# Narrowing the weights four slices ahead instead of two in a recurrence and feed-forward kernel, with a new order for its first third

## The chip, the cores and the metric

The kernel runs on one core of one Trainium2 chip. The metric is device time in microseconds (us) of one execution; a time for the kernel is the median of several runs. A second kind of number comes from the profile of one single execution, whose own time is given beside its span (the stretch that the profiler's records cover).

## What is computed

A recurrence over 768 steps for 4 x 8 heads of width 40 (RWKV-7), whose output becomes the 3072 x 320 input of an RMS norm and a SwiGLU feed-forward with 1536 inner columns:

```python
batch, n_heads, seq, head_dim = (4, 8, 768, 40)
for t in range(S):
    kt, vt, rt = (k[:, :, t], v[:, :, t], r[:, :, t])
    wt, at, bt = (w[:, :, t], a[:, :, t], b[:, :, t])
    y[:, :, t] = np.einsum('bhd,bhde->bhe', rt, state)
    Sa = np.einsum('bhde,bhe->bhd', state, at)
    state_decay = state * wt[:, :, None, :] - np.einsum('bhd,bhe->bhde', Sa, bt)
    state = state_decay + np.einsum('bhd,bhe->bhde', vt, kt)
...
x = np.ascontiguousarray(attn_out.transpose(0, 2, 1, 3)).reshape(B * S, H * D)
rms = np.sqrt(np.mean(x * x, axis=-1, keepdims=True) + 1e-06)
xn = x / rms * rms_g
g = xn @ w_gate
silu = g * (1.0 / (1.0 + np.exp(-g)))
val = xn @ w_val
return (silu * val @ w_out).astype(np.float32)
```

The weights w_gate, w_val and w_out arrive as 64-bit numbers.

## The kernel before

**Tiling.** The 768 steps are cut into 24 chunks of 32. Each chunk passes three stages. `front(c)` (L652) loads w, a, k, b and v of the chunk, turns them on TensorE and builds, level by level (pieces of kind `gramk`), the triangular matrix `LT` and the scaled keys `KN` and decays. `inverse(c)` (L760), or `early_inverse(c)` (L778) for the first four chunks, inverts the triangular matrix on VectorE by a chain of small multiply and subtract pairs; the matrix goes through DRAM to change its layout, out by `sB<-LT` and in by `M<-sB` before the chain, and out by `sY<-M` (or `sY<-Yi`) and back after it. In the early form two TensorE pieces of kind `inv` follow, which need the four loads `M<-sY`. `main(c)` (L810) takes the state from chunk to chunk (kinds `state`, `lower`, `update`), forms the outputs (`score`, `level`, `y0`), and normalises them into `xg`; with `main` of an even chunk go the `rn` loads of r for two chunks.

After each second chunk `feed(g)` (L939), g = 0 to 11, applies the feed-forward to the 256 tokens of two chunks. It goes over the 12 slices f of 128 inner columns in six pairs; a pair loads two slices of weights (`wf<-sW`, 480 KB each; "load f" below), then runs the TensorE pieces `h64`, `h` and `out` with ScalarE's silu and VectorE's product in between.

**The narrowing.** The 64-bit weights become 32-bit on chip, once, while the first chunks run. `narrow_slice(f)` (L995) does slice f in two halves, stages "narrow 2f" and "narrow 2f + 1", so there are 24 halves, 0 to 23 ("half 11" is the second half of slice 5). `narrow` (L973) loads raw weights into a wide buffer by two or four DMAs, makes three ScalarE instructions and three VectorE instructions of it, and stores the result to the DRAM scratch `sW[f]`, from which all twelve groups load.

**Wide buffers.** There are WB = 5 of them, named `wf`. A turn counter gives them out in rotation, in the order in which the Python code asks: for the raw halves and for the feed loads alike. So a request waits for whatever read the buffer five requests before. In `feed(0)` the requests interleave:

```python
for f in range(LEAD if g == 0 else 0):
    narrow_slice(f)
for f in range(0, FT, 2):
    for e in range(2):
        if g == 0 and f + LEAD + e < FT:
            narrow_slice(f + LEAD + e)
```

and then the pair's two loads are asked for. With LEAD = 2 halves 0 to 7 come first, then loads 0 and 1, halves 8 to 11, loads 2 and 3, and so on; loads 8 to 11 come last.

**What sets the order.** Nothing is issued while the Python code of the stages runs. The helpers (`dve` and its kin at L442 to L489) only record a piece: its engine, its kind and what it must wait for. `Plan.issue` then issues the 6028 pieces in the order that the string ORDER (L33) spells out: each number is a piece's distance from the first one not yet issued, and "-" is a warm-up matmul (L1015), 151 in all, which keeps TensorE busy and whose result is not used. Each engine, and each of the DMA queues of SyncE (SP) and GpSimd (POOL), does its own pieces in this order and waits at each for what that piece needs. The places given below count the pieces of one engine, from 0. PAIRS (L228) says for each of 499 rooms (a use of PSUM by one result) which of three pairs of PSUM banks, `ps0` to `ps2`, it lives in; the feed-forward's output sums in `po`.

All helpers record from one line each, so most VectorE work stands under L444 in the profile, ScalarE copies under L467, scalings under L470, other ScalarE work under L464, DMAs under L483 and matmuls under L486 and L489; what tells them apart is the tile.

Of the kernel before, what the change touches and what calls it, by code (L numbers as in the profile page):

```python
# [22 lines left out]
LEAD = 2  # L23
# [10 lines left out]
85 83 84 76 58 78 86 74 73 59 60 75 5 89 61 88 77 4 43 6 201 7 87 334 90 44 8 214 213 53 62 9 - - - - - - - - 93 18 10  # L34
567 335 557 11 12 13 79 14 15 94 566 80 210 16 95 558 108 17 200 - - - 97 96 19 20 100 21 2 22 101 23 98 25 568 202 24
26 107 112 57 - - - - - 102 106 111 124 27 209 122 392 103 109 52 119 113 104 54 578 569 577 155 199 125 110 105 204
120 - - - - - - 114 203 118 117 121 559 211 598 589 562 46 131 129 132 45 560 212 597 563 588 561 123 115 136 586 384
133 134 - - - - - 126 130 116 47 564 3 145 216 394 383 135 336 128 137 48 144 143 141 91 587 219 142 51 570 127 1005
565 146 138 337 55 573 579 281 393 220 582 608 571 390 234 239 607 572 583 580 380 574 251 222 38 221 609 575 581 42 -
- - - - - - - 223 82 226 339 64 379 227 338 39 81 139 224 263 149 576 238 153 56 249 247 590 206 584 228 382 237 591  # L40
593 272 40 233 232 381 154 0 593 32 139 390 204 228 591 388 234 249 247 - - 324 235 35 31 27 244 229 146 147 259 281
245 258 149 34 325 594 36 33 270 155 243 62 605 584 598 230 - 239 40 214 599 601 242 628 64 49 91 627 602 30 626 1135
600 28 48 257 603 29 241 68 150 255 65 0 1347 194 0 194 84 173 0 - - - 182 540 200 0 184 1 186 542 540 0 506 0 457 469
849 199 455 242 111 97 110 112 96 51 61 439 460 458 122 50 243 0 0 255 242 0 709 104 470 242 120 246 259 708 57 247
458 456 0 257 718 256 470 242 0 716 265 487 486 0 268 0 0 265 101 473 0 262 277 0 273 0 236 0 260 0 269 0 242 461 - -
- - - - - 237 0 240 0 278 242 252 0 242 252 0 90 0 0 98 99 246 0 0 230 440 0 230 94 93 457 440 231 - - - - - - - - -
240 441 244 0 44 0 468 440 255 0 450 468 269 469 0 257 214 439 238 213 203 0 257 203 93 449 92 0 0 234 - - - - - - - -
245 437 0 250 262 0 464 246 247 436 260 245 446 258 259 469 244 - - 255 471 465 468 470 466 0 269 215 255 478 466 93
94 264 95 96 266 97 0 97 470 1 2 98 99 0 0 96 467 97 469 98 468 251 265 99 470 100 471 101 441 102 103 258 104 105 260
106 - - - - - - - - - - - 0 106 107 471 108 0 108 502 503 472 0 108 109 110 111 0 0 0 0 0 - - 13 0 16 562 572 146 571  # L50
561 147 14 142 143 374 15 13 355 - - - 25 386 358 0 358 386 388 16 25 387 389 390 70 79 17 391 28 191 147 355 356 80
148 149 359 0 68 28 2 29 149 0 149 34 150 29 151 187 24 25 31 152 33 153 188 391 393 32 154 35 390 392 358 0 0 152 40
187 153 27 154 155 156 33 157 158 159 160 161 34 162 36 163 164 37 165 41 391 38 42 392 39 394 561 166 395 393 552 0
42 559 549 548 395 209 0 549 560 42 165 210 43 44 211 427 428 395 - - - 565 166 45 167 557 168 0 565 566 168 739 0 522
693 534 526 124 - - 0 526 124 139 0 535 681 682 579 0 535 545 547 140 536 138 141 0 547 545 555 543 578 0 558 520 567
- - - - - - 518 378 0 696 378 380 381 695 518 120 685 526 - - - - - - 522 686 379 527 382 136 530 383 554 529 121 - -
141 540 523 565 539 537 142 538 524 - - - - 145 525 148 534 149 152 154 551 535 147 555 - - 157 146 550 536 150 155
# [3 lines left out]
478 595 568 - - 35 830 594 567 820 38 36 - 476 37 571 366 570 0 605 356 433 434 435 436 120 437 0 317 318 319 320 441  # L61
321 322 323 355 456 324 458 459 442 4 357 325 457 326 327 443 328 0 443 328 329 330 331 357 0 35 0 330 2 37 450 359 3
36 358 331 332 357 333 356 0 462 330 461 464 448 331 332 468 364 447 463 31 467 476 458 333 365 334 335 0 425 439 441
302 426 436 0 6 439 2 0 435 332 2 436 443 444 0 448 332 442 334 443 333 340 449 0 32 297 329 342 330 - 3 338 33 341
334 0 332 331 0 332 293 441 0 438 0 436 293 333 336 295 337 309 438 338 1 375 342 310 365 374 515 27 292 0 362 26 28
44 339 29 34 292 27 32 338 0 646 29 34 336 32 0 439 64 315 647 646 339 440 441 63 340 0 287 413 312 313 623 12 414 314
415 315 416 608 624 32 417 480 418 625 419 420 421 316 626 638 33 0 312 417 625 418 - - - - 476 313 601 602 600 610
812 419 420 421 822 258 422 423 0 313 810 423 625 637 2 0 819 2 0 254 473 420 421 645 310 422 0 - - - - - 310 422 3
313 33 0 28 626 307 419 639 627 420 637 308 0 637 20 635 420 647 21 421 23 422 613 648 819 38 22 809 423 39 659 24 611
3 612 36 818 424 651 808 621 425 25 660 426 - 616 249 427 0 427 3 25 58 57 428 28 47 0 428 429 28 430 3 431 0 26 25  # L70
614 484 31 27 617 627 0 458 216 400 590 600 401 0 12 582 32 401 583 25 0 397 579 21 - - - - - - - - - 588 29 28 30 591
22 453 428 398 605 23 0 591 23 429 602 24 609 0 24 397 588 602 1 604 398 429 430 2 399 427 0 584 - - - - - - - - - - -
- - - 4 397 0 25 397 4 0 393 394 21 23 27 28 395 598 24 424 607 0 21 38 35 395 37 396 24 2 424 47 397 398 399 400 25
# [4 lines left out]
663 729 634 977 562 563 717 713 986 978 665 564 565 566 975 567 568 714 569 985 570 571 967 722 572 723 - 0 400 403  # L78
726 402 572 401 573 0 726 738 736 573 739 574 664 575 737 576 577 3 723 578 751 579 760 580 747 581 582 633 583 584 0
584 585 3 634 586 636 587 635 734 588 633 0 746 588 - - - - - 403 757 589 722 590 3 404 591 592 593 594 595 596 408  # L80
# [288 lines left out]
def kernel(  # L369
# [569 lines left out]
    def feed(g):  # L939

        x = xg.pop(g)
        po = po_
# [6 lines that stand above are left out]
            plan.stage = "feed", g  # L949
# [98 lines left out]
```

## Time and profile before

| | us |
|---|---|
| three runs | 1069.33, 1063.34, 1067.66 |
| median | 1067.66 |
| the profiled execution, own time | 1062.36 |
| its span | 1060.6 |
| mean granted TensorE clock in it | 0.979 of full |
| PE busy | 1009.5 (95%) |
| PE weight load busy | 829.3 (78%) |
| DVE busy | 842.3 (79%) |
| ACT busy | 468.1 (44%) |
| POOL busy | 309.5 (29%) |

PE is TensorE, DVE is VectorE, ACT is ScalarE, POOL is GpSimd and SP is SyncE, which here does nothing but start DMAs. The profile gives for each instruction its start, its duration, the tile that it writes and reads, and what ended the idle time before it. A view by windows cuts the span and gives each engine's busy time in each piece, and the clock that TensorE was granted (1.00 is full).

The six largest groups after the matmuls are these; those with `ex`, `wf` and `sW` belong to the narrowing and the feed loads.

| group | count | busy us or median |
|---|---|---|
| PE ps<-xg,wf, the feed-forward's first product | 1728 | 353.5 us |
| PE po<-wf,hT, its second | 576 | 183.1 us |
| DVE tmp<-Yi,M and Yi<-Yi,tmp, the inverse's chain | 1240 | 260.4 us |
| DVE K<-K,T | 192 | 93.4 us |
| ACT K<-K | 168 | 71.7 us |
| DMA wf<-sW | 144 | 3.9 us from issue to landing |

### The profile page before, as it was taken

How to read it: one execution, taken by the hardware profiler on the slowest of the kernel's cores; microseconds unless marked ns; L12 is line 12 of the kernel's file. 1: busy time of each engine (PE TensorE's matmuls, PEld its weight loads, DVE VectorE, ACT ScalarE, POOL GpSimd, SP SyncE). 2: the span in 40 equal slices, each digit the busy share in tenths (PEclk: the TensorE clock that was granted, in tenths of full speed). 3: DMA queues.
4: the chain of work that ended last, by engine and by line, in shares of the span. 5: the costliest groups of instructions: out<-in, count | busy, mean ns of one | idle time of the engine just before them, and what ended most of it. 6: DMA issues, size and time to landing. Idle time of an engine off the chain costs nothing.

```text
span 1060.6 us, 53494 instructions
## 1 busy us (share of the span) xinstructions
PE 1009.5 (95%) x23406; PEld 829.3 (78%) x23406; DVE 842.3 (79%) x2861; ACT 468.1 (44%) x1043; POOL 309.5 (29%) x554
## 2 busy tenths in 40 slices
PE   7868999999999999999999999999999999999997
PEld 6767777777888778787778778787777888787875
DVE  8978878776868988898898798989889899787411
ACT  6856666643543534434443444434344443431211
POOL 8824413120532241241233241340331331110000
PEclk9777998999999999999999999999999999999999
DMA  9965458766565483655565555574555555443252
GB/s 168 216 155 133 77 127 207 211 123 178 127 140 126 106 173 96 150 134 125 123 155 129 135 132 114 122 160 119 137 126 126 138 137 138 100 132 102 80 162 68
DMA packets 172457, 143.35 MB, mean 135 GB/s; under 512 B 125504, under 2 KB 143872, under 8 KB 172224
## 3 DMA queue, kind: packets, MB, share of 16 engines
q1 hardware_dynamic: 153856, 116.96, 42.9%
q0 software_dynamic: 16192, 22.64, 12.1%
q8 instruction: 184, 3.01, 1.2%
q10 hardware_dynamic: 2176, 0.33, 0.3%
q14 instruction: 49, 0.40, 0.1%
HBM read 123.86 MB, written 15.99 MB: 132 GB/s over the span
## 4 chain that ended last, share of the span: by engine, by line
PE 72%; DVE 8%; DMA 4%; ACT 3%; issue 3%; POOL 2%; SPq 1%; DVEq 0%; ACTq 0%; POOLq 0%
PE ps L486 50%; PE po L486 13%; PE ps L489 8%; DMA wf<-sW 2%; DVE LT L444 1%; DVE y L444 1%; DVE tmp L444 1%; POOL kbn L483 1%; DVE Yi L444 1%; DVE K L444 1%; SPq L483 1%; DMA sY<-Yi 1%; ACT VU L467 1%; PE po L1015 0%; DVE Ab L444 0%
## 5 line engine op out<-in xcount | busy, mean ns | idle before, releaser
L486 PE MATMUL ps<-xg,wf 128*128 128x256 f32 (+1 forms) x1728 | 353.5, 390 | 4.0 <-DVE xg L444 2.0
L486 PEld LDWEIGHTS ps<-xg,wf 128*128 128x128 f32 (+1 forms) x1728 | 261.4, 188 | 57.2 <-issue 15.0
L486 PE MATMUL po<-wf,hT 128*128 128x320 f32 x576 | 183.1, 449 | 0.1
L464 ACT ACTIVATE sg<-ps 128x256 f32<-128x256 f32 x144 | 53.6, 382 | 228.2 <-PE ps L486 224.9
L444 DVE TENSOR_TENSOR tmp<-Yi,M 128x60 f32<-128x60 f32 (+24 forms) x620 | 130.7, 211 | 19.1 <-DMA M<-sB 5.9
L444 DVE TENSOR_TENSOR Yi<-Yi,tmp 128x60 f32<-128x60 f32 (+24 forms) x620 | 129.7, 209 | 12.7
L483 POOL DMA_DIRECT2D VU<-in_v_dram x92 | 53.2, 584 | 274.1 <-PE ps L486 141.8
L486 PEld LDWEIGHTS po<-wf,hT 128*128 128x128 f32 x576 | 102.5, 191 | 35.7 <-issue 4.1
L444 DVE TENSOR_TENSOR hT<-ps,sg 128x256 f32<-128x256 f32 x144 | 59.7, 420 | 67.2 <-ACT sg L464 66.4
L444 DVE TENSOR_TENSOR K<-K,T 128x512 f32<-128x512 f32 (+1 forms) x192 | 93.4, 496 | 8.3 <-PE ps L486 5.8
L486 PEld LDWEIGHTS ps<-Ab,K 40*64 40x64 f32 x4608 | 77.2, 138 | 28.1 <-issue 10.5
L467 ACT COPY K<-K 128x256 f32<-128x256 f32 (+1 forms) x168 | 71.7, 443 | 58.4 <-PE ps L486 39.2
L486 PE MATMUL ps<-Ab,K 40*64 40x56 f32 x4608 | 87.2, 224 | 9.7 <-issue 3.8
L444 DVE TENSOR_TENSOR As<-ps,msi 128x256 f32<-128x256 f32 (+1 forms) x186 | 78.9, 476 | 14.4 <-PE ps L486 13.8
L467 ACT COPY KN<-ps 128x640 f32<-128x640 f32 x96 | 66.1, 690 | 53.5 <-PE ps L489 23.3
L483 POOL DMA_DIRECT2D kbn<-in_b_dram x92 | 53.3, 583 | 96.7 <-PE ps L486 94.3
L486 PEld LDWEIGHTS ps<-As,KN 128*40 128x40 f32 x3072 | 66.5, 124 | 15.7 <-issue 10.4
L483 POOL DMA_DIRECT2D kbn<-in_k_dram x92 | 53.6, 585 | 82.7 <-PE ps L486 82.6
L486 PE MATMUL ps<-As,KN 128*40 128x32 f32 x3072 | 73.2, 205 | 3.1 <-issue 2.5
L483 POOL DMA_DIRECT2D wn<-in_w_dram x92 | 51.6, 567 | 62.7 <-DVE tmp L444 24.1
L444 DVE TENSOR_TENSOR y<-y,ps 128x256 f32<-128x256 f32 x119 | 50.0, 420 | 16.2 <-PE ps L486 13.7
L444 DVE COPY_PREDICATED LT<-near,ps 128x384 f32<-128x384 uint32 (+2 forms) x72 | 52.2, 725 | 2.6 <-PE ps L486 2.0
(133 smaller groups left out, 1546.0 us busy)
## 6 DMA issues: line engine op xcount, KB each, us to landing
wf<-sW SPq DMA_DIRECT2D x144, 480.0 KB, 3.9
M<-sB SPq DMA_DIRECT2D x80, 128.0 KB, 4.1
rn<-in_r_dram SPq DMA_DIRECT2D x24, 160.0 KB, 5.4
sW<-ex SPq DMA_DIRECT2D x16, 240.0 KB, 3.4
out_dram<-o SPq DMA_DIRECT2D x48, 80.0 KB, 4.2
kbn<-in_k_dram POOLq DMA_DIRECT2D x92, 40.0 KB, 3.9
kbn<-in_b_dram POOLq DMA_DIRECT2D x92, 40.0 KB, 4.1
wan<-in_a_dram POOLq DMA_DIRECT2D x46, 80.0 KB, 4.9
```

The source lines that it names most:

```text
L444: plan.add("DVE", kind, lambda at: fn(at(o), *m(at)), [o], aps(*args))
L464: plan.add("ACT", "act", lambda at: nc.scalar.activation(at(o), at(a), f, **kw), [o] + aps(acc), [a])
L467: plan.add("ACT", "copy", lambda at: nc.scalar.copy(at(o), at(a)), [o], [a])
L483: plan.add(by, "dma", lambda at: queue.dma_start(out=o, in_=i), [o], [i])
L486: return o, lhsT, rhs, lambda at: nc.tensor.matmul(at(o), lhsT, rhs, start=start, stop=stop, skip_group_check=True)
L489: return o, i, ident, lambda at: nc.tensor.transpose(at(o), i, ident)
```

## The change

Three things are edited. LEAD goes from 2 to 4; ORDER is written anew; PAIRS is written anew.

```diff
-LEAD = 2
+LEAD = 4
...
 ORDER = """
-85 83 84 76 58 78 86 74 73 59 60 75 5 89 61 88 77 4 43 6 201 7 87 334 90 44 8 214 213 53 62 9 - - - - - - - - 93 18 10
...
 PAIRS = """
-0120112210001221012012210211000102102120201021100221210111012202202000111100112120100012102221212201000112001120122221
...
+0120112210001001102012210202122202101220101012200002002222121011110121211100220202200021111200102022000211022221211200
```

LEAD changes no piece, only when a slice is asked for. Halves 0 to 11 now ask for their buffers first, then loads 0 and 1, halves 12 to 15, loads 2 and 3, halves 16 to 19, loads 4 and 5, halves 20 to 23, and then loads 6 to 11. With five buffers in rotation, this is what each request of `feed(0)` follows in its buffer:

| request | before, follows | after, follows |
|---|---|---|
| loads 0, 1 | halves 3, 4 | halves 7, 8 |
| halves 8, 9, 10 | halves 5, 6, 7 | halves 3, 4, 5 |
| half 11 | load 0 | half 6 |
| half 15 | load 2 | load 0 |
| half 19 | load 4 | load 2 |
| half 23 | load 6 | load 4 |
| loads 2, 4 | loads 1, 3 | loads 1, 3 |
| load 6 | load 5 | load 5 |
| load 8 | load 7 | half 21 |
| loads 3, 5, 7 | halves 8, 12, 16 | halves 12, 16, 20 |
| loads 9, 10, 11 | halves 20, 21, 22 | halves 22, 23, load 6 |

The new ORDER has as many entries as before (6179) and the same number of warm-ups. Its last 4129 entries name the same pieces in the same order as before. On PE the pieces from place 113 up to the last 718 of 1056 are arranged differently, most of them by a few places; on the other engines the order differs almost from the start, up to about 285 us on DVE and 313 us on ACT and POOL. The line numbers of the changed kernel are higher by one from PAIRS on.

More of the change, by code (lines that the diff above doesn't have):

```diff
@@ new lines @@
+75 43 87 - - - - - - - - 93 202 94 96 95 100 101 108 62 45 111 48 112 558 567 27 334 2 90 29 578 557 569 589 577 214
+56 200 57 568 566 209 335 - - - 97 98 107 106 109 - - - - - 102 103 104 113 201 34 119 199 210 124 122 559 55 105 110
+91 586 79 588 80 587 123 117 - - - - - - 114 115 125 562 563 129 118 579 120 560 580 570 - - - - - 126 121 137 130 68
+69 46 204 211 573 135 383 203 392 47 54 384 212 38 67 71 134 561 564 565 571 116 581 136 128 131 132 336 582 133 127
+144 141 597 609 92 219 1005 145 390 337 220 234 138 139 574 146 572 221 575 226 227 143 590 222 142 393 379 72 381 339
@@ new lines @@
+338 591 149 3 81 598 583 593 584 239 28 594 251 238 - - - - - - - - 223 263 153 224 394 155 49 380 249 228 608 576 150
+33 627 154 140 233 232 607 272 247 237 35 229 235 230 236 585 82 606 148 - - 325 205 215 391 147 231 - 240 248 592 245
+156 250 599 36 389 600 246 595 262 602 260 243 603 244 601 326 604 610 611 259 256 261 151 152 1006 605 1 628 241 638
+- - - 252 99 613 270 255 257 271 242 612 258 269 254 268 267 208 218 31 40 37 382 157 158 159 160 399 401 400 402 253
+614 615 161 406 162 163 164 165 414 166 407 418 618 629 617 0 326 586 607 618 596 566 249 387 389 234 236 400 398 397
@@ new lines @@
+160 45 567 208 161 162 383 0 415 416 383 162 579 - - 45 163 164 571 165 0 26 25 0 682 119 120 121 122 123 537 138 0
+162 524 534 535 0 547 559 521 543 568 545 0 - - - - - - 518 138 137 545 139 519 0 527 526 542 530 553 529 - - - - - -
+522 135 523 366 158 - - 141 696 687 695 688 686 537 369 538 524 367 142 540 525 - - - - 145 146 370 554 120 677 292
+368 153 149 148 534 - - 157 152 552 535 147 550 536 565 539 155 154 165 164 371 160 150 680 681 10 682 121 161 151 162
+549 0 1 0 548 553 0 44 0 2 0 0 429 37 41 42 43 506 508 509 507 44 45 420 421 432 436 422 434 437 571 553 449 566 559
@@ new lines @@
+563 0 434 432 563 45 571 0 571 572 563 445 165 442 166 584 436 441 439 45 573 576 46 577 575 448 47 446 440 48 574 49
+11 0 0 431 575 0 429 - - 35 36 38 585 37 568 478 567 574 573 584 571 0 562 0 0 678 430 428 669 203 677 668 411 412 417
+425 426 433 445 281 282 283 284 285 286 287 288 667 8 13 2 - 323 289 324 413 454 290 213 291 0 426 13 824 659 669 325
+291 8 292 428 440 9 326 330 329 328 293 10 658 213 203 47 45 421 11 825 294 295 296 422 437 14 297 443 327 339 423 438
+441 340 433 439 0 73 46 296 297 298 299 440 300 301 302 44 303 432 434 450 433 304 305 306 446 0 306 446 447 307 12
@@ new lines @@
+442 340 53 443 451 452 308 454 453 347 346 0 0 426 411 427 318 310 - 22 1 308 309 320 415 0 310 313 319 314 309 21 274
+423 421 422 420 293 275 349 359 317 315 70 276 277 278 294 25 358 348 279 324 325 499 320 321 322 326 0 21 2 3 22 322
+0 24 0 0 18 627 297 298 5 6 32 0 28 610 609 314 414 14 415 15 56 315 416 316 417 317 418 627 628 419 318 319 484 27
+420 421 422 423 1 424 2 642 26 612 621 - - - - 485 320 629 630 0 631 422 644 318 423 319 608 616 0 423 424 425 631 618
+33 32 0 19 401 616 402 617 403 404 626 405 406 628 407 630 408 642 409 294 238 239 458 295 - - - - - 296 629 29 30 602
@@ L233 @@
-210020201010100100012102102
+0120112210001001102012210202122202101220101012200002002222121011110121211100220202200021111200102022000211022221211200
+2221212111100220121102202211200202200222111111002020220202212100220122212211000011100012222101111211201100000001200202
+1000110010201212112020222200110120200022112011111200110101111002011111002222021212002022110111202011221101120112222020
+0202001102211211111020021222122200000200002100021011111122010100221020011000122210221100011002211111012111122202101222
@@ L234 @@
+201121210101011011102012012
 """
```

59 lines of the change are left out of this document (17 added, 42 removed), and 303 rows, old and new, of the table ORDER.

## The prediction

> **What bounds the kernel now.** I began with the slices of the span (busy tenths of PE and the clock it was granted) and the chain that ended last.
>
> ```profile
> PE   7868999999999999999999999999999999999997
> ...
> PEclk9777998999999999999999999999999999999999
> ...
> PE 72%; DVE 8%; DMA 4%; ACT 3%; issue 3%; POOL 2%; SPq 1%; DVEq 0%; ACTq 0%; POOLq 0%
> ```
>
> TensorE sets the end. It is below full work only in the first four slices (a slice is 26.5 us), and there, and once more near 180 us, its clock is cut. Only that part can give anything back, so I read it in windows of 20 us (columns: length, busy time and count by engine, granted clock, DMA share, GB/s).
>
> ```profile
> 20.00:40.00 20.00, 14.78 (x344) 12.61 (x336) 18.62 (x40) 17.92 (x37) 17.46 (x39) 0.82 0.84 174
> 40.00:60.00 20.00, 18.42 (x360) 16.68 (x362) 19.66 (x71) 17.16 (x36) 11.30 (x22) 0.76 0.88 205
> 60.00:80.00 20.00, 13.24 (x354) 11.80 (x347) 13.37 (x47) 9.21 (x19) 2.98 (x7) 0.76 0.67 163
> 80.00:100.00 20.00, 17.64 (x653) 15.85 (x655) 16.95 (x58) 10.70 (x23) 8.74 (x16) 0.73 0.55 146
> 160.00:180.00 20.00, 18.69 (x454) 15.10 (x454) 19.31 (x75) 13.58 (x31) 8.68 (x15) 0.91 0.91 233
> 180.00:200.00 20.00, 19.60 (x405) 16.53 (x399) 14.59 (x45) 14.29 (x29) 0.00 (x0) 0.92 0.60 177
> 400.00:420.00 20.00, 19.83 (x587) 16.00 (x588) 17.89 (x61) 8.67 (x20) 2.30 (x4) 1.00 0.44 115
> ```
>
> From 20 to 100 us PE idles 15.9 of 80 us (80 less 14.78, 18.42, 13.24 and 17.64). The missing clock, (0.18 + 0.24 + 0.24 + 0.27) x 20 x 2, is 37 us at half rate, and 6.8 us more lie in 160 to 200. At 400 us PE idles 0.2 of 20. Third, the list of PE's waits from 20 to 320 us gives the stalls a name (total, times, longest).
>
> ```profile
> PE ps L486 <- DVE tmp L444: 4.9, 2, 4.2
> PE ps L486 <- ACT KN L467: 2.2, 1, 2.2
> ...
> PE ps L489 <- ACT x L470: 0.8, 1, 0.8
> ```
>
> The 4.2 us is the start of `inverse` 0 on PE, at 70.95. The releaser named is DVE, but SyncE's queue (start, duration) shows a DMA behind it.
>
> ```profile
> 60.40 0.30 SPq L483 DMA_DIRECT2D sY<-M  x1
> 60.75 0.66 SPq L483 DMA_DIRECT2D sW<-ex  x1
> ...
> 63.65 1.29 SPq L483 DMA_DIRECT2D sY<-M  x1
> ...
> 67.17 1.85 SPq L483 DMA_DIRECT2D M<-sY  x4
> ```
>
> The second half of the store `sY<-M` stands behind a store and four loads of the narrowing (60.75 to 63.60); only after it do the four `M<-sY` loads go, and PE waits for them.
>
> **What the change leaves alone.** The pieces are the same 6028 and the warm-up matmuls the same 151, so no instruction is added or removed. PE's order is the same for its first 113 pieces and its last 718 of 1056 (from about 280 us), DVE's for its last 2093 of 2858, SyncE's for its last 445 of 696. The line of PSUM pairs looks all new, but of 499 rooms only 52 follow another room in their pair, the last in `front` 7; the rest is renamed. I price the rooms and everything past 285 us at nothing: PE is 99% busy there, which covers it; without that cover one room's wait costs what such waits cost before, 0.2 to 0.8 us.
>
> **LEAD and the buffers.** Half 11 of the narrowing waited for the reader of the first group's load 0, on PE; now it follows half 6. Its four loads, issued from 136.44 to 140.78, are SyncE's 87th to 116th place instead of 121st to 124th, and go by about 122 us. Halves 15, 19 and 23 now wait for the readers of loads 0, 2 and 4 instead of 2, 4 and 6. The first two feed loads pay for it: they went at 46.70 and 55.30, and now stand in SyncE's places 69 and 73, behind halves 7 and 8. They are wanted at 130.27 by `feed` 0's first h64, so some 60 us cover the delay: nothing. Without it each landing is 3.9 us (median of 144). Loads 2 and 4 still wait for loads 1 and 3 and cost what they did.
>
> **The early third, step by step** (against the profiled execution, 1062.36 us with a span of 1060.6).
> 1. SyncE stood idle from 19.75 to 23.60 for GpSimd's memset of `wn`, which moves from GpSimd's place 35 to 13; behind it `main` 0's first matmul waited 2.24 us for the KN copy of `front` 0 (ended 33.78). But that copy had stood 1.44 us behind half 3's loads on ScalarE, and DVE is 93% busy in this window. Between 0 and -2.2; I take -0.5, nearer to the full engines.
> 2. `inverse` 0: the second `sY` store moves from SyncE's place 72 to 66, ahead of the half 6 store and all but one of half 9's loads: 60.75 to 63.65 is 2.9 us. DVE's chain ahead of it is done at place 143 instead of 151. Against that, feed load 1 with its wait for half 8 stands between the four `M<-sY` loads. Between 0 and -4.2; I take -2.7.
> 3. The clock behind that gap. Windows of 4 us show it (same columns).
>
> ```profile
> 68.00:72.00 4.00, 0.79 (x64) 0.71 (x64) 3.69 (x15) 1.78 (x4) 0.42 (x1) 0.80 0.82 201
> 72.00:76.00 4.00, 2.88 (x99) 2.47 (x100) 1.58 (x9) 0.96 (x3) 0.00 (x0) 0.50 0.77 215
> 76.00:80.00 4.00, 3.55 (x45) 3.15 (x45) 0.45 (x2) 2.91 (x6) 1.55 (x4) 0.50 0.45 51
> ```
>
> From 72 to 80 PE was busy 6.43 us at half rate; at full rate at best half of it, -3.2. It may also come back elsewhere: the stretch of 6.8 us near 180 cost at most its half, +3.4. The matmuls there are short and wait for ScalarE in between, so I take -1. The Trainium skill ("TensorE: Matmul & The Clock Gate", Part 1) has the array fall to half rate after a free-running window of about 3.4 us without work; the row 68 to 72 agrees, but near 180 it does not: from 172 to 176 PE was busy 3.04 of 4.00 us, and the next window shows 0.53. By that rule alone this step would give -3.2 and the sum -4.1.
> 4. At 103.01 a turn of `front` 3 had waited 0.80 us for ScalarE's scale of x, which stood behind three VU copies of 0.42 each; now it stands ahead of them. PE cannot gain more than its wait: -0.8, bounds 0 and -0.8.
> 5. GpSimd now has `front` 4's kbn loads (first issue 114.48, after `main` 1's level is done) ahead of the memset of `inverse` 2 (106.06), and SyncE's four `M<-sY` of `inverse` 2 (107.07) wait for that memset. They move to about 117 to 118.8; `inverse` 0's ended at 69.02 and PE went at 70.95, 1.9 us later, so PE's `inv` at 121.63 has some 0.9 us left, and the two rn loads behind them on SyncE (117.80) are wanted only two chunks on. The kbn loads end some 1.7 us later, because memsets and other loads of 0.6 us stand between them. Between 0 and +1.7; I take the middle, +0.8.
> 6. Near 180 us, where DVE is 97% busy: half 23's first load now waits at SyncE's place 159 for load 4's reader, `out` of `feed` 0's third pair, which ended at 179.16. Before, half 19's last load waited for it.
>
> ```profile
> 174.13 0.98 SPq L483 DMA_DIRECT2D wf<-in_moe_w_out_dram  x1
> 175.16 0.44 SPq L483 DMA_DIRECT2D wf<-in_moe_w_gate_dram  x1
> ...
> 179.19 0.38 SPq L483 DMA_DIRECT2D wf<-in_moe_w_val_dram  x1
> ```
>
> Behind the waiting one now stand both loads of half 20 (174.13 and 175.16 above), half 17's store, two loads of half 19 (170.53 and 171.70 before) and feed load 6 (182.84 before). ScalarE takes halves 20 and 19 in order (0.74 + 0.70 + 0.60 us each) ahead of four VU copies of `main` 3, which had ended at 190.48; 2.9 us of issues ahead of half 19's loads (0.38 + 0.98 + 0.44 + 0.41 + 0.74), 3.9 for the landing, 4.1 for the halves and 1.7 for the copies, with 1.1 for other copies between, put their end 13.7 us after 179.16 where it was 11.3. Between 0 and +4; I take +2.3.
>
> Sum: -0.5 - 2.7 - 1 - 0.8 + 0.8 + 2.3 = -1.9, or 1060.5 for an execution like the profiled one. That one lies 5.3 us under the median of the three runs (1067.66); the mean of all four times (1069.33, 1063.34, 1067.66, 1062.36) is 1065.7, and from it I forecast **1063.8**. About 0.5%, 5.3 us, is what a measurement of this kernel can tell from no change.
>
> **Rivals.**
> A. The early stalls really go: `inverse` 0's whole 4.2, the clock's 3.2, 0.5 and 0.8, and neither step 5 nor 6 shows: -8.7, **1057.0**. For it: 7.4 of the 8.7 sit on one DMA that is now issued early. Against: DVE is 93 to 98% busy from 20 to 60, so the next wait is close behind.
> B. Slower: the queue head of step 6. If the VU copies end some 4 us later, PE, which had come to them straight from its warm-up matmuls, idles as long as at 66.74 to 70.95 (4.21), and the clock may halve behind it as it did there for 10.2 us, of which at most 5.1 are lost: +9.1, and with half of the early gain kept (-4.2 / 2), +7.0, **1072.7**. It decides from some 3.4 us of idle. For it: SyncE, ScalarE and DVE each run in one order, and DVE is full there. Against: half 19 no longer waits for 179.16 with its last load alone, and can land as early as before.
> C. The order does not tell: what comes early waits for the next full engine (DVE at 160 to 183, without a gap), and all is taken back before 200 us: 0, **1065.7**.
>
> **How the numbers follow.** Forecast 0.40, A 0.32, B 0.20, C 0.08. Forecast and most of C (0.05) are no change, A is faster, B and the rest of C slower: 0.32, 0.45, 0.23. All lower bounds together are -2.2 - 4.2 - 3.2 - 0.8 = -10.4, all upper ones 3.4 + 1.7 + 4 = +9.1: from 1065.7 that is 1055.3 to 1074.8, and my range is 1055.5 to 1074.5. The likeliest case alone reaches from 1060 to 1068.
>
> **What will show it.** Step 1: a shorter wait for KN near 32 us. Step 2: PE's wait at `inverse` 0 under 2 us. Step 3: a clock above 0.5 behind it. Step 4: no wait for x in `front` 3. Step 5: `M<-sY` of `inverse` 2 near 117. Step 6: SyncE waiting with half 23's load for the end of `out`, halves 20 and 19 behind it, and PE idle between the warm-ups and `feed` 0's fourth pair. I am wrong if DVE waits where it was full before 60 us, if the half-rate stretches move to places with long matmuls, or if PE's idle time past 280 us changes by more than 1 us.

## The result, and the profile after

| | before | after |
|---|---|---|
| median of 16 runs each | 1064.39 us (1060.09 to 1076.8) | 1071.46 us (1064.55 to 1076.47) |
| ratio, 95% interval | | 1.0062 [1.004, 1.0085] |
| profiled execution, own time | 1062.36 | 1073.42 |
| its span | 1060.6 | 1071.6 |
| mean granted clock | 0.979 | 0.976 |

The change makes the kernel slower, by 0.62% of 1064.39, about 6.6 us. The ratio is not the quotient of the two medians: it goes by the executions within 1.5% of the fastest of their kernel. First the slices and the chain of the changed kernel, the views that open the prediction.

```profile
PE   6768898999999999999999999999999999999998
...
PEclk9886999999999999999999999999999999999999
...
PE 74%; DVE 8%; DMA 6%; issue 4%; ACT 3%; SPq 2%; POOL 2%; ACTq 0%; DVEq 0%; POOLq 0%
```

As before, TensorE sets the end and only the first slices are below full work. The same windows of 20 us (length, busy time and count of PE, PE load, DVE, ACT, POOL, then granted clock, DMA share, GB/s):

```profile
20.00:40.00 20.00, 14.58 (x405) 12.47 (x404) 17.64 (x47) 17.06 (x37) 10.96 (x23) 1.00 0.84 179
40.00:60.00 20.00, 16.53 (x310) 15.15 (x309) 17.64 (x64) 12.31 (x25) 12.17 (x26) 0.74 0.64 148
60.00:80.00 20.00, 12.00 (x326) 11.01 (x325) 16.42 (x54) 11.72 (x26) 5.46 (x11) 0.74 0.75 192
80.00:100.00 20.00, 16.46 (x541) 14.80 (x541) 13.40 (x41) 11.23 (x21) 4.61 (x10) 0.64 0.50 124
160.00:180.00 20.00, 17.01 (x403) 14.03 (x398) 14.54 (x52) 8.58 (x21) 8.73 (x15) 0.91 0.53 145
```

From 40 to 60 us ScalarE does 12.31 us of work where it did 17.16, VectorE 17.64 where it did 19.66, and PE 16.53 where it did 18.42: engines that were full now wait. The list of PE's waits from 40 to 80 us names what for.

```profile
PE ps L487 <- DVE tmp L445: 4.0, 1, 4.0
PE ps L487 <- DVE K L445: 2.3, 1, 2.3
PE ps L490 <- ACT K L468: 1.7, 1, 1.7
PE ps L487 <- issue: 1.4, 2, 1.0
PE ps L487 <- DVE M L445: 0.8, 1, 0.8
```

Before, this list held one long wait, 4.2 us at `inverse` 0. That one is gone; four others, 4.0 + 2.3 + 1.7 + 0.8 = 8.8 us, have come, all ahead of it, in the last pieces of `front` 1 and `front` 2. PE's own time line shows where (start, duration, work, idle time before and its releaser), first before:

```profile
59.24 1.56 PE L486 MATMUL ps<-Ab,K 40*64 40x56 f32 x64
...
62.01 1.16 PE L486 MATMUL ps<-Ab,K 40*64 40x56 f32 x64 [0.56 <-DVE K L444]
...
70.95 0.79 PE L486 MATMUL ps<-M,LT 16*16 16x16 f32 x64 [4.21 <-DVE tmp L444]
```

and after:

```profile
57.14 1.16 PE L487 MATMUL ps<-Ab,K 40*64 40x56 f32 x64 [0.84 <-DVE M L445]
...
62.63 1.16 PE L487 MATMUL ps<-Ab,K 40*64 40x56 f32 x64 [2.34 <-DVE K L445]
...
68.47 1.97 PE L487 MATMUL ps<-Ab,K 40*64 40x56 f32 x64 [4.04 <-DVE tmp L445]
70.80 1.62 PE L490 MATMUL ps<-ident,K 104*128 104x104 f32 x8 [0.36 <-DVE M L445]
72.21 4.15 PE L1016 MATMUL po<-ident 128*128 128x128 f32 x22
76.29 0.69 PE L487 MATMUL ps<-M,LT 16*16 16x16 f32 x64
```

The last `gramk` of `front` 2 runs at 68.47 where it ran at 62.01. So PE comes late to its warm-ups, the first of the two `inv` pieces follows them without a wait, and it starts at 76.29 where it started at 70.95.

What makes `front` 2 late is read from ScalarE and VectorE. ScalarE first, around the last halves of the narrowing that are now in front of it:

```profile
54.17 0.41 ACT L468 COPY K<-K 128x256 f32<-128x256 f32 x1 [0.84 <-PE ps L487]
56.80 1.39 ACT L465 ACTIVATE ex<-wf,ctop 128x480 f32<-128x480 int16 x2 [2.23 <-DMA sW<-ex]
58.22 0.69 ACT L465 ACTIVATE ex<-ex,cmid 128x480 int32<-128x480 f32 x1
...
61.47 0.82 ACT L468 COPY K<-K 128x256 f32<-128x256 f32 x2
...
67.23 0.68 ACT L468 COPY KN<-ps 128x640 f32<-128x640 f32 x1
```

Half 6's first instruction stands 2.23 us, until half 3's store has freed the `ex` buffer. That store moved from SyncE's place 52 to 58 and was issued at 50.80. Behind it stand halves 7 and 8 and, at 61.47, a K copy of `front` 2 which before ran at 51.69:

```profile
51.69 0.81 ACT L467 COPY K<-K 128x256 f32<-128x256 f32 x2
```

VectorE tells the same further on:

```profile
63.41 0.66 DVE L445 SCALAR_TENSOR_TENSOR ex<-wf,ex 128x480 f32<-128x480 f32 x1 [0.93 <-ACT ex L465]
...
66.69 0.66 DVE L445 SCALAR_TENSOR_TENSOR wf<-wf 128x480 f32<-128x480 uint32 x1
67.46 0.66 DVE L445 SCALAR_TENSOR_TENSOR o<-wf,o 128x480 f32<-128x480 f32 x1
68.03 0.28 DVE L445 TENSOR_TENSOR Ab<-Ab,T 128x128 f32<-128x128 f32 x1
```

The piece `Ab` of `front` 2, which the last `gramk` reads, moved from VectorE's place 146 to 159. Before, it ran at 57.84:

```profile
57.84 0.27 DVE L444 TENSOR_TENSOR Ab<-Ab,T 128x128 f32<-128x128 f32 x1
```

Now it stands behind halves 6 to 8 and runs at 68.03, 0.44 us ahead of the `gramk`. PE's wait is put down to a `tmp` of VectorE, its neighbour there.

A second piece held the same `gramk`. In its room of PSUM it now follows the last turn of `front` 1, where before it followed the first `gramk` of `front` 2. The reader of that turn is `front` 1's `KN` copy (67.23 in the rows of ScalarE above), and it moved from ScalarE's place 74, where it ran at 46.41, to 92, behind halves 6 to 8. It ends at 67.91, and `Ab` at 68.32, so here `Ab` comes last, by 0.4 us.

The queue of SyncE, for the step that the prediction leaned on:

```profile
62.31 0.63 SPq L484 DMA_DIRECT2D sY<-M  x1
...
65.36 0.32 SPq L484 DMA_DIRECT2D wf<-sW  x1
...
66.95 0.41 SPq L484 DMA_DIRECT2D M<-sY  x1
68.15 0.32 SPq L484 DMA_DIRECT2D wf<-sW  x1
68.52 0.42 SPq L484 DMA_DIRECT2D M<-sY  x1
...
70.13 0.86 SPq L484 DMA_DIRECT2D M<-sY  x2
```

The second `sY` store does go earlier, 62.31 for 63.65. But feed loads 0 and 1 (65.36 and 68.15, which wait for halves 7 and 8) now stand around the `M<-sY` loads, and the last of these landed at 75.66.

How far PE is behind the profile of before, at the start of the same piece, in two profiles taken of the changed kernel and a second one of before:

| piece on PE | before, at | after | after, again | before, again |
|---|---|---|---|---|
| `front` 1, last `gramk` | 45.96 | +1.5 | +3.0 | +0.6 |
| `front` 2, last but one | 59.24 | +3.4 | +5.1 | -1.1 |
| `front` 2, last `gramk` | 62.01 | +6.5 | +9.6 | +1.3 |
| `main` 0, first piece behind the `inv` pair | 74.25 | +4.5 | +8.2 | +0.7 |
| `inverse` 2, first `inv` | 121.63 | +5.2 | +11.0 | +0.8 |
| `feed` 0, third pair | 167.44 | +11.3 | +15.3 | +1.4 |
| `feed` 0, fourth pair | 190.53 | +8.6 | +14.9 | -1.8 |
| `main` 5 | 297.73 | +6.7 | +14.0 | +0.3 |
| end of the span | 1060.6 | +11.0 | +14.0 | -0.6 |

At 211 us PE is 5.4 and 12.0 us late, and 4.5 and 8.2 of that were there by 75. What is added between 127 and 167 us and partly given back up to 211 differs between the two, and so does the rest: past 297.73 the first profile loses 4.3 us more, the second nothing.

### The profile page after: what moved, and what is told of

It reads as the page before. It is cut to its first block, busy times and chain, and to the rows that moved or that the text cites. A ratio compares the mean times of both kernels' runs of the same rounds, so it can differ in the third digit from the quotient of the medians.

```text
span 1071.6 us, 53471 instructions
## 1 busy us (share of the span) xinstructions
PE 1009.8 (94%) x23406; PEld 829.9 (77%) x23406; DVE 843.6 (79%) x2861; ACT 466.8 (44%) x1043; POOL 308.4 (29%) x554
## 4 chain that ended last, share of the span: by engine, by line
PE 74%; DVE 8%; DMA 6%; issue 4%; ACT 3%; SPq 2%; POOL 2%; ACTq 0%; DVEq 0%; POOLq 0%
PE ps L487 51%; PE po L487 14%; PE ps L490 9%; SPq L484 2%; PE po L1016 2%; DMA kbn<-in_b_dram 1%; POOL kbn L484 1%; DVE tmp L445 1%; DVE LT L445 1%; DMA wf<-sW 1%; DVE K L445 1%; DVE y L445 1%; DVE Yi L445 1%; DMA wn<-in_w_dram 1%; ACT K L468 1%
```

## The experiments

The first question is which part of the change costs: the new places, or LEAD with its rotation of buffers. "Places" are those of one engine's pieces. Unless said otherwise a kernel's time is its ratio to the kernel before with the 95% interval, over 6 to 12 runs.

### LEAD alone, the new order alone

```diff
-LEAD = 2
+LEAD = 4
 # ORDER as before, but for what the new rotation forces on SyncE
-loads 0, 1, 7, 9, 10 at places 63, 58, 163, 178, 184
+loads 0, 1, 7, 9, 10 at places 66, 71, 170, 183, 191
```

> LEAD = 4 with the order of before; only the feed loads move, to the first place on SyncE at which their buffer is free (load 1 from place 58 to 71, load 0 to 66, three later ones by 5 to 7). Theory 1 (the loss comes from SyncE's queue: feed loads 0 and 1 now wait for halves 7 and 8 and hold up inverse 0's DMAs behind them): load 0 holds the queue until half 7 is done (62.4) and load 1 until half 8 is (64.7), the second sY store goes near 65.4 instead of 63.65, PE starts inverse 0 near 72.7 instead of 70.95, time 1.5 to 2 us over before, ratio 1.0015 to 1.002. Theory 2 (the loss comes from the new order of ScalarE and VectorE, where halves 6 to 8 stand ahead of front 2's last levels): as before within 0.5 us but for the same 1.75 at inverse 0; front 2's last gramk starts near 62.0 as before. Theory 3 (the loss is in where half-rate stretches happen to fall): no relation; ratio anywhere from 0.997 to 1.006.

```diff
-LEAD = 4
+LEAD = 2
 # ORDER as after, but for what the old rotation forces on SyncE
-loads of half 11 at places 87 to 116, of half 15 at 123 to 128
+loads of half 11 at places 119 to 122, of half 15 at 134 to 147
 # and one load each of halves 19 and 23, and load 8, 5 to 12 places later
 # half 9's gate load at 71 instead of 56; two ScalarE and one VectorE piece of half 11 7 to 11 places later
```

> LEAD = 2 with the new order; pieces whose buffer is not yet free are put off to the first place where it is (halves 11, 15, 19 and 23 go back to where before had them, the rest stays). Feed loads 0 and 1 now follow halves 3 and 4, long done, and hold nothing up; the store of half 8 still stands between the four M<-sY loads. Theory 1: PE starts inverse 0 near 74.4 instead of 76.29, ratio to before 1.004 instead of 1.0062. Theory 2: front 2's last gramk stays near 68.5 and what follows stays 4 to 6 us later than in before, ratio 1.004 to 1.006. A ratio under 1.002 would say that LEAD itself, not the order, costs the time.

Measured: LEAD alone 1.0074 [1.0041, 1.0108], as slow as the whole change. `inverse` 0 came at 72.46, near what its first theory had, but no theory had so slow a kernel. The new order with LEAD = 2 came to 1.0244 [1.0199, 1.029], but it is no clean test: ScalarE stood 4.25 us at half 11 at 147.82, which the new order has ahead of a VU copy that PE waits for, and there PE went from +8.5 to +16.6 us. No theory had 1.0244 either, nor `inverse` 0 at 78.57. So LEAD, priced at nothing, is not free; of the places e2 says little.

### The queue against the order of VectorE and ScalarE

Two causes can make `inverse` 0 late: SyncE's loads among the four `M<-sY`, or PE's own lateness out of `front` 2. First the queue alone, then both.

```diff
 # SyncE, from the second sY store on
-half 9's out load, half 6's store, load 0, half 9's two val loads, M<-sY, load 1, M<-sY, half 10's gate load, half 8's store, M<-sY x2
+half 9's out load, half 6's store, half 9's two val loads, M<-sY x4, loads 0 and 1, half 10's gate load, half 8's store
```

> The changed kernel with four DMAs of SyncE moved: feed loads 0 and 1, half 10's first load and half 8's store go behind inverse 0's four M<-sY loads instead of between and ahead of them. Theory 1: the loads go from 66 to 68, land near 71, and PE starts inverse 0 as soon as it is through front 2's last turn (72.4) instead of at 76.29; 3.5 to 4 us are saved there and kept, ratio 1.0025 to 1.003. Theory 2: the same start, since front 2's end at 72.4 is what then holds PE, some 1.5 us later than in before; if front 2's chain is the true limit further on, less than 2 us of it are kept. Theory 3: no relation.

```diff
 # as e3, and: VectorE, pieces 56, 57 and 62 (Ab) of front 2
-behind halves 6 to 8
+ahead of half 6's last piece; 68 ahead of half 8
 # ScalarE, copies 59, 63, 69 and 70 of front 2
-behind half 8
+ahead of half 8's pieces
```

> As the run with the loads behind, and in addition five DVE pieces of front 2's last levels (two K, Ab, and the last K) and four ScalarE copies of it go ahead of parts of halves 6 to 8 instead of behind them. Theories 1 and 2 together: front 2's last gramk starts near 64 instead of 68.5, inverse 0 near 71 instead of 76.29; 5 us are saved, ratio 1.000 to 1.002. Theory 1 alone: no more than the run with the loads behind. Theory 3: no relation.

```diff
 # as e4, and: copies 46, 58, 59 and 63 of front 2 on ScalarE, 44, 45, 56, 57 and 62 on VectorE
-behind pieces of half 6
+ahead of half 6's (46, 44, 45 first of all)
```

> The run with loads behind and front 2's pieces earlier, and in addition front 2's K pieces of the level before (two VectorE, one ScalarE) ahead of half 6, and the last level's ahead of halves 6, 7 and 8. Theory 2 (the order of ScalarE and VectorE around front 2 is what the new order costs): front 2's last but one gramk starts near 60.5 instead of 62.6, the last near 63 instead of 68.5, and inverse 0 at 71 to 71.5 as its loads land (70.75), so the start of main 0 is back at what before had; if that was all, ratio 1.000 to 1.002. If it stays at 1.004 or more with inverse 0 at 71, the rest is lost behind it: at feed load 7, or in the instruction fetches.

```diff
 # VectorE and ScalarE as in e6, SyncE as in the changed kernel
```

> The run with front 2 first without its four moves on SyncE: the VectorE and ScalarE pieces of front 2 stand early, but feed loads 0 and 1 stand again among inverse 0's M<-sY loads and wait for halves 7 and 8, which are now later themselves. If both had to be mended together: the last M<-sY load lands at 75 to 77 as in the changed kernel, PE starts inverse 0 at 75.5 to 77, and nothing of the 4 us is kept, ratio 1.005 to 1.007. If the order of VectorE and ScalarE alone was the cause: inverse 0 near 72 to 73, ratio as with both, 1.002.

```diff
 # as e6, and in front 1: ScalarE's copy 59 right behind 58, VectorE's where 66 some places earlier
```

> The run with front 2 first, and two more pieces of the same kind: ScalarE's second K copy of front 1's level 8 ahead of half 5's last piece (VectorE waited 1.64 us for it, and PE 1.67 us ahead of front 1's last turn), and VectorE's last where of front 1 ahead of inverse 0's later steps (PE's second gramk of front 2 shares its PSUM pair and waited 0.84 us for it). Theory 2 again: the start of front 1's last turn 1 to 1.3 us earlier, front 2's second gramk 0.8 us earlier on top, ratio 0.999 to 1.001, no slower than before. If nothing is gained at inverse 0 because its M<-sY loads set it, ratio stays at 1.002.

Measured (lateness of PE against the profile of before):

| | ratio [95%] | last `gramk` of `front` 2 | `main` 0 behind the `inv` pair |
|---|---|---|---|
| after | 1.0062 [1.004, 1.0085] | +6.5 | +4.5 |
| e3, queue alone | 1.0118 [1.0066, 1.017] | +7.8 | +5.4 |
| e9, order alone | 1.0038 [1.0007, 1.0068] | +4.3 | +5.1 |
| e4, both | 1.0047 [1.0009, 1.0085] | +4.4 | +1.3 |
| e6, both, more | 1.0022 [0.9996, 1.0048] | +4.6 | +2.2 |
| e10, and `front` 1 | 1.0042 [1.0009, 1.0075] | +3.7 | +0.6 |

In e3 the last `M<-sY` landed at 70.26, 5.4 us earlier than after, and PE was no earlier: it came out of `front` 2 late. In e9 it came out earlier, and then:

```profile
69.66 3.71 PE L1016 MATMUL po<-ident 128*128 128x128 f32 x22
73.50 0.20 PE L487 MATMUL ps<-M,LT 16*16 16x16 f32 x2
76.48 0.86 PE L487 MATMUL ps<-M,LT 16*16 16x16 f32 x62 [2.78 <-DMA M<-sY]
```

Two matmuls of the `inv` run at 73.50 and the other 62 wait 2.78 us for the loads. In e6, with both mended, the `inv` waits for nothing:

```profile
69.96 4.09 PE L1016 MATMUL po<-ident 128*128 128x128 f32 x22
73.98 0.69 PE L487 MATMUL ps<-M,LT 16*16 16x16 f32 x64
```

So two waits lie side by side and end within a microsecond of each other (75.66 and 76.29 after): taking away either gives nothing, both together 2.3 to 3.9 us at this place. At the end, all four kernels other than e3 lie below the changed kernel, by 0.0015 to 0.004, but no interval is clear of its. That the early loss reaches the end is shown as a tendency, not one by one.

None of the four brings the last `gramk` back. It was expected near 64 in e4 and near 63 in e6, and came at 66.41 and 66.62; e4, e6 and e10 are all slower than the 0.999 to 1.002 expected of them, e6 by the least, and so is e3 than its 1.003. What is left is the room. This is the `gramk` of e6:

```profile
66.62 1.97 PE L487 MATMUL ps<-Ab,K 40*64 40x56 f32 x64 [3.83 <-ACT KN L468]
```

In e4, e6, e9 and e10 the `Ab` and K pieces of `front` 2 were ready by 62.2 to 64.2. The `KN` copy of `front` 1, which none of them moves ahead of the halves, ended at 66.35, 66.56, 66.27 and 65.67, and PE began the `gramk` 0.05 to 0.06 us behind it each time, after a wait of 1.4 to 3.8 us. So three things hold up this stretch, not two. What the kernel would gain with that copy or that room put back is not shown: no run does it.

### What of LEAD costs

```diff
 # e1, and on SyncE
-loads 0 and 1 ahead of inverse 0's second sY store, load 3 at place 92
+loads 0 and 1 behind inverse 0's M<-sY, load 3 behind inverse 1's
```

> LEAD = 4 with the order of before, as the first run, but feed loads 0, 1 and 3 stand where they never hold SyncE's queue: 0 and 1 right behind inverse 0's four M<-sY, 3 behind inverse 1's. Theory A (the waits of feed loads for halves 7, 8 and 12 are what LEAD costs): PE starts inverse 0 near 71 again instead of 72.5 and the 0.7 us near 100 go too; 2.2 us and what hangs on them are saved, ratio 1.003 to 1.005 where the first run had 1.0074. Theory B (LEAD costs where the later halves stand: feed load 7 now follows half 20 and lands at 198 us, behind the fourth pair's h64 at 197): h64 of the fourth pair still stops for its second buffer, ratio not under 1.004. Theory C (the loss is in PE's pauses at instruction fetches, which come every 128 matmuls and grow with the DMA traffic): ratio as in the first run, 1.006 to 1.008, with pauses of 0.7 to 3 us at the same instructions.

```diff
-LEAD = 4
+LEAD = 2
 # every engine's order as in e1: loads 0, 1, 7, 9, 10 late, but waiting for what they waited for before
```

> LEAD = 2 and the order of before, but with SyncE's feed loads 0, 1, 3, 7, 9, 10 and 11 at the places of the first run (LEAD = 4 with the old order), so that all five engines have exactly its order and only the buffers differ. If the late feed loads are what LEAD costs: as slow at feed 0's fourth pair (h64 stops for load 7 near 197), ratio 1.003 to 1.007. If the rotation costs (half 11's loads, no longer held by feed 0's reader, go at 130 instead of 136 and 140; feed loads held by halves 7, 8 and 12): inverse 0 at 71 as in before, ratio 1.000 to 1.002.

Measured: e5 1.0046 [1.0023, 1.0068], e15 0.9991 [0.9963, 1.0018]. e15 and e1 (1.0074) differ in nothing but which use each wide buffer follows, and their intervals are apart: late loads cost nothing that shows, the rotation is what costs. e5 cannot be told from e1. (e1 and e15 ran on different chips, each beside the kernel before.) How it costs is mostly not seen. One place is: in e1 load 7 waits for half 20 and goes at 193.30, and the first `h64` of the fourth pair, which reads it, stops after four matmuls (the releaser named, a VectorE piece, had nothing to do with it).

```profile
196.65 0.70 PE L486 MATMUL ps<-xg,wf 64*128 64x256 f32 x4 [0.40 <-ACT VU L467]
198.17 2.63 PE L486 MATMUL ps<-xg,wf 64*128 64x256 f32 x12 [0.82 <-DVE Yi L444]
```

In e15 the same 16 matmuls run from 188.74 without that stop. Second profiles were taken of before, after, e1, e5 and e15.

> The kernel before once more, for a second profile of the same program. PE's pauses without a releaser should stand at the same instructions (471 matmuls in, 850, 1231, 1487, 4030, 4668 and so on) if they are instruction fetches, with other lengths; the starts of inverse 0 (70.95), of feed 0's fourth pair (190.53) and of front 7's first piece should come within 2 us of the first profile.

> The changed kernel once more. If the order is the cause, front 2's last gramk starts again near 68.5 and inverse 0 near 76.3. The pause of 2.99 us at 160.72 stands at the same instruction if it is a fetch; if it is gone or short, that part of the profiled loss (about 4 us with the half-rate stretch behind it) was this execution's.

> LEAD = 4 with the old order, second profile. If feed load 7 behind half 20 is a steady cost: h64 of feed 0's fourth pair stops again for 0.8 us at its second buffer, 197 us in. If SyncE's hold at feed loads 0 and 1 is: inverse 0 again 1.5 us later than in e15 or before. If the pauses at instruction fetches between 125 and 185 us are what costs: they are again longer than in the two profiles of before, at the same instructions.

> LEAD = 4, old order, feed loads 0, 1 and 3 late, second profile. Steady costs: h64 of the fourth pair stops again for load 7 (1.0 us in the first profile). The half-rate stretch of 10 us at 135 us and the pauses of 1.7 us at 72 and 77 us were this execution's if they are gone.

> LEAD = 2 with the first run's order on all engines, second profile: feed 0's fourth pair starts within 2 us of before's 190.53 and does not stop inside h64; time from 1061 to 1069.

Their times were 1061.86, 1076.34, 1071.59, 1071.2 and 1070.54. The stop shows in all four profiles of e1 and e5 (0.3 to 1.0 us), at most 0.1 in e15's two, and not in the changed kernel. PE runs 51 to 62 us at half rate before 300 us in e1 and e5, 34 and 44 before, 44 and 48 after, 24 and 55 in e15. One such stretch, 10.2 us at 132 to 135 us, lies on the first long matmuls of `feed` 0 in e5's two profiles and e1's second, and PE falls 4.2 to 4.8 us further behind there. The rest of what the rotation costs, 5 us or so, stays open: two profiles of one kernel differ by as much. e15's second profile was expected near its first and was not: though the `h64` did not stop, its fourth pair came 2.7 us late, and at `main` 5 PE was 7.2 us behind before, as far as in e1's first. So it is the ratios that speak against the rotation, not the profiles. The changed kernel's second profile, too, was later than expected, with the `gramk` at 71.56 and `inverse` 0 at 80.08.

### The moved store by itself, and the warm-ups

```diff
 # before; on SyncE
-second sY store at place 72, first M<-sY at 77
+second sY store at place 67, first M<-sY at 73
```

> The kernel before (LEAD = 2, its own order) with SyncE's second sY store of inverse 0 moved from place 72 to 67 and the four M<-sY loads from 77 to 73: the one step that the prediction priced at -2.7. If the price was right and the step alone is missing its conditions in the changed kernel: the loads go near 65, land near 69, and PE starts inverse 0 at 68.8 instead of 70.95, ratio 0.998. If a wait stands right behind (VectorE's and ScalarE's work ahead of main 0): inverse 0 early, the start of main 1's first piece as before, ratio 1.000.

Measured: `inverse` 0 at 67.86, 3.1 us earlier than before; at 115 us PE was still 1.7 us ahead. The ratio is 1.0017 [0.9979, 1.0055], which does not tell a small gain from none: in the profiled execution a half-rate stretch of 10.2 us at 127.5 took the gain away by 139 us.

```diff
 # e12: e3, with 2 of the 11 warm-ups just ahead of inverse 0's inv
-- - - - - - - - - - -
+- -
```

> The run with the loads behind, with 2 instead of 11 warm-up matmul pieces ahead of inverse 0's first matmuls. There PE came out of front 2 at 73.8, ran the 11 warm-ups until 77.2 at half clock although the loads had landed at 70.3, and started only then. If the warm-ups, in the way of a PE that is late, are what it lost: inverse 0 starts 2.5 to 3 us earlier than in that run (near 74), and half of it or more is kept. If the clock drops longer for their lack, that shows as more half-rate time from 70 to 100 (10 us before), and it is given back.

```diff
 # e13: e12, and nine warm-ups more ahead of the fourth pair of feed 0
+- - - - - - - - -
```

> The run with fewer warm-ups, but the nine that were left out ahead of inverse 0 stand ahead of feed 0's fourth pair (23 there instead of 14), so that from about 200 us on every matmul has the same number in PE's stream as in before. If the loss of 29 us comes from where PE's instruction fetches fall (a pause at every 128th matmul): the pauses past 285 us stand at the old instructions again and sum to 11 to 15 us instead of 23, and the ratio is 1.003 to 1.012 instead of 1.0287 (the nine cost up to 4 us at the new place). If the loss comes from the clock or from work that is late after inverse 0: ratio stays over 1.02.

```diff
 # e14: before, with the same nine left out
-- - - - - - - - -
```

> The kernel before without nine of the 11 warm-up pieces ahead of inverse 0, where PE then waits for loads anyway (idle 4.2 us, then about 8). By the fetch theory: no gain at inverse 0, pauses at other instructions from there to the end, ratio 1.015 to 1.03. If the loss was one of the changed kernel's order only: ratio under 1.005.

Measured: e12 1.0287 [1.0245, 1.0328], e13 1.0028 [0.9995, 1.006], e14 1.0189 [1.0144, 1.0233]. (In the profile each of these float32 warm-ups is two matmuls, so eleven show as x22.) e12's loss was not expected; e14, which repeats it in before, was. Leaving out nine small matmuls makes the kernel slower by 0.017 (e12 less e3) or 0.019 (e14), some 18 to 20 us. In e12 the `inv` did start 3.4 us earlier than in e3, of which 1.4 were left behind it, and at 190 us PE was even 1.8 us ahead of before; the loss comes later, up to +25. It is no wait for another engine. These are the first lines of PE's waits past 285 us, of before, e12, e13 and e14 in this order.

```profile
PE ps L486 <- issue: 7.4, 13, 1.3
```

```profile
PE ps L486 <- issue: 17.9, 18, 2.7
```

```profile
PE ps L487 <- issue: 4.1, 6, 1.4
```

```profile
PE ps L486 <- issue: 23.8, 16, 3.5
```

"issue" is time in which PE waited for nothing that the profile shows: 10 to 16 us more with nine warm-ups fewer, and back when as many are put in elsewhere (e13 has two such lines more, of 1.4 us each, so 6.9 us in all). The clock is halved past 500 us as well, for 17.1 us in all in e14 and 10.2 in e12, not at all in before and e13 but for their last microseconds. e13 is better than e3, and their intervals do not meet (again on different chips); in its profile PE is 1.4 us ahead of e3's at 115 us and 4.1 at 190. In e3 the eleven warm-ups, put there to fill a wait, had become the wait. Why e3 should be slower than the changed kernel, if it is, no run shows.

## Why the prediction was wrong

The forecast was 1063.8, 1.9 us less than the 1065.7 that it started from; measured is 1071.46, 6.6 us more, inside the range by the side that had 0.23. It is near rival B's 1072.7, but that is luck, for B's mechanism did not happen: among the warm-ups ahead of the fourth pair PE idled 0.98 us (197.79), no 4.2, and no engine was named for it.

- **Step 2 is the step that failed** (-2.7 at `inverse` 0; measured +5.3 there and +4.5 behind it). Its price was right for what it priced: e11 does only that move and gains 3.1. Wrong was to take it from the times of before and to ask only what ended last there. The same edit put halves 6 to 8 ahead of `front` 2's `Ab` and K copies, and half 3's store behind six others; none of these ended a long wait before, so none was priced, though the order shows each. `front` 2's last `gramk` came 6.5 us late, and PE with it. The prediction did name feed load 1 among the `M<-sY`, and this alone would have eaten the gain (e9), had PE not been later still.
- **LEAD at nothing** failed too: e1 1.0074, against e15 0.9991. The reason given (60 us of cover for loads 0 and 1) holds for when their data are wanted, but not for SyncE's queue, in which a waiting load holds up what stands behind it: `inverse` 0 comes at 72.46 and 75.36 in the two profiles of e1, at 71.48 and 69.93 in e5, and at 70.95 and 71.69 before. What the rotation does elsewhere was not looked at.
- **The rooms at nothing** failed as well, and by more than any wait of 0.2 to 0.8 us. `front` 2's second `gramk` (57.14) now follows `front` 1's last in its room, whose reader moved on VectorE from place 127 to 133: 0.84 us. And `front` 2's last `gramk` follows `front` 1's last turn, whose reader moved on ScalarE from 74 to 92. In the changed kernel `Ab` hides that wait; in e6 it is 3.83 us by itself. The cover named, PE's work past 285 us, does not reach this place.
- **Step 1** (-0.5): the long wait for `KN` is gone, as said, but `main` 0's first matmul starts 0.7 and 1.0 us later, before again 1.9 later. No gain, none lost that could be told.
- **Step 3** (-1): the clock behind the gap is 1.00 at 76 to 80, but the warm-ups ahead of it now run at half rate. Half-rate time before 300 us is 44.4 in both first profiles: 0.
- **Step 4** (-0.8): the wait is gone and PE goes from +5.0 just ahead to +4.1, and from +9.3 to +8.3 in the second profile, -1.0 in both: right. But a pause with no releaser inside the same turn (0.83 and 1.86 us) takes it back: +5.0 and +10.3 behind it.
- **Step 5** (+0.8): the mechanism is right, the size under half. `M<-sY` went at 122.46 to 125.40, near 117 plus PE's lateness, and PE waited for them 0.33 and 0.38 us inside the `inv`. That PE goes from +4.5 to +5.2 and from +9.9 to +11.0 up to the start of the `inv` looks like the price, and is luck: it lies ahead of those loads, 0.71 and 0.62 us of it a wait for VectorE's y.
- **Step 6** (+2.3): from +8.7 at the third `out` to +8.6 at the fourth pair; +15.2 to +14.9: nothing. The reader was wrong: half 23's first load waited for the third pair's `h` (ended 181.77, load 181.80), not for `out` (189.17). It held the queue 1.5 us, and no cost of it reached the fourth pair.

The sum that the runs support: +4.5 to +8.2 by 75 us from order, queue, rooms and rotation together, steps 4 to 6 about nothing, and up to 5 us either way from half-rate stretches and pauses that differ between executions. How the measured 6.6 us divides is not settled: the rotation alone (e1) costs as much as all of it, mending the places gives back some 1.6 to 4.3 us (0.0015 to 0.004), the places without the rotation could not be had cleanly (e2), and the room of `front` 1's turn was never given back by itself.

## What to carry to other kernels

When pieces are moved forward on in-order engines, price first those that are put behind them, on each engine and in each buffer and room, by when their readers want them; the wait that ended last before tells only what can be gained. Two waits that end together hide each other, so an experiment has to take away both, and then look for a third. Keep the number of matmuls in such a comparison, and take a second profile before a pause or a slow stretch is put down to the edit.

## What was not expected of the hardware

- **Pauses of PE with no releaser.** They are up to 3.5 us long. Of those over 0.4 us, 10 of before's 17 and 14 of after's 19 come back at the same matmul in the second profile, many of them 128 matmuls (with their 128 weight loads, 256 instructions) apart. The longest after is at 160.72; the same instruction in the second profile waited 0.57:

```profile
159.50 1.22 PE L487 MATMUL ps<-As,KN 128*40 128x32 f32 x53
163.72 0.42 PE L487 MATMUL ps<-As,KN 128*40 128x32 f32 x11 [2.99 <-issue]
```

  The page's queue of instructions has 184 packets for PE's 46812 matmuls and loads, 254 each:

```profile
q8 instruction: 184, 3.01, 1.2%
```

  The Trainium skill ("Runtime: NRT & Kernel Launch", Instruction fetch mechanics) has an engine's instructions fetched in blocks of 256 and the cost of a boundary mostly hidden. The packets and the spacing agree, and mostly holds too: before has 184 packets and 17 pauses over 0.4 us, 15.1 us in all. What is not hidden is what counts here. The traces tie the pauses to the packets: one comes every 5.8 us on average, and each of before's 17 pauses and of e14's 23 ends 2.2 to 3.2 us behind the start of one, as do 16 of after's 19. The nine warm-ups fit this. Seven of e14's 23 pauses stand at the same count of PE's matmuls as in before, six of them behind the 18 that are left out, so they fall 18 matmuls later in the work. Why they are longer there, no run shows.
- **A VectorE instruction beside a memset.** In e3 a TENSOR_SCALAR of 0.40 us took 1.52 while GpSimd wrote `ST` (66.79 to 67.76).

```profile
66.51 1.52 DVE L445 TENSOR_SCALAR wf<-wf 128x480 int32<-128x480 int32 x1
```

  The Trainium skill ("SBUF — State Buffer", Who interferes with whom) says that this form of instruction can take a port pair that GpSimd shares, and that whichever is issued second is then blocked until the other is done. The row agrees in length, ending 0.27 us behind the memset; but by the records VectorE's began first, so it is not shown which of the two was issued second.
- **Half rate behind work.** In e11 the clock is halved from 127.5 us on, behind a window in which PE was busy 3.25 of 4.00 us with 142 short matmuls:

```profile
123.00:127.00 4.00, 3.25 (x142) 2.72 (x141) 3.99 (x11) 3.23 (x10) 3.98 (x8) 1.00 0.60 103
127.00:131.00 4.00, 3.74 (x77) 3.16 (x78) 2.58 (x12) 1.74 (x5) 1.66 (x3) 0.56 0.38 66
```

  PE's longest idle in the 6.8 us ahead of 127.5 was 0.57 us. No idle of several us is needed, then, and the same program has such stretches at other places in another execution.
